# A linear-attention and feed-forward kernel: all chunks in pairs, decay folded into q and k, one written order for all work

## The chip, the cores and the metric

The kernel runs on one core of a Trainium2 chip. The core has five engines with an instruction queue each: PE (TensorE, matrix products into PSUM), DVE (VectorE), ACT (ScalarE), POOL (GpSimd) and SP (SyncE, which here only issues DMAs). Instructions of one engine run in the order of its queue; engines wait for each other through semaphores. The metric is the device time of one execution in microseconds (us). Before the change three runs took 216.35, 214.18 and 216.23 us, median 216.23.

## The reference

A causal attention without softmax, in which each head h forgets with a factor lam[h] per position, is followed by a two-layer network with ELU. The reference works in blocks of 64 positions; what it computes per head is

```python
intra = (qb @ kb.T) * Dmask          # Dmask[i, j] = lam ** (i - j) for i >= j, else 0
intra = intra @ vb
inter = (qb * lam_pow) @ kv_state    # lam_pow[i] = lam ** (i + 1)
out[block] = intra + inter
kv_state = lam ** block * kv_state + (kb * rev_pow).T @ vb   # rev_pow[j] = lam ** (block - 1 - j)
# then, with x = out as [3072, 512]:
h = x @ w_in                         # [3072, 2048]
g = where(h > 0, h, exp(min(h, 0)) - 1)
return g @ w_out                     # [3072, 512]
```

Batch 4, 8 heads, 768 positions, head size 64; inputs and output are float32, the kernel works in fp16 with float32 sums in PSUM.

## The kernel before, in words

The 3072 rows are 24 chunks of 128 positions: chunk g is position block g // 4 of batch g % 4. A chunk depends on the chunk four before it through the state of its batch.

For one chunk the program has these steps, each a small function. q, k and v are loaded by POOL's DMA queue with a cast to fp16 (`emit_load`, line 109), chunks 0 to 3 one by one, later ones two at a time; q of chunk 0 comes by SP's queue and is cast by DVE. T: q and k are transposed, for chunks 0 to 7 on PE (`att_T_pe`, 283), with q multiplied by the decay `qs` on its way out of PSUM (DVE, 290) and k copied by ACT (291); for later chunks by DMA transposes on SP's queue (`att_T_dma`, 268), straight from the loaded tiles. S: 16 matmuls give the scores (302). E: DVE multiplies them by `mask`, which holds the causal pattern and a decay per column (318). P: the values (338) and, from chunk 4 on, the state (344) are summed in PSUM, and ACT (359) or DVE (361) copies the result to `xt`. POOL makes the decayed k, `kd` (174), not for chunks 20 to 23. U: kd times v is the addition to the state (397 or 406); POOL has multiplied the old state by the block's decay into `stt` (378), and DVE adds the two (416, 418).

The network follows as units. mm1 of a group of chunks (`1:g:j`, line 478) puts 512 columns into one of two PSUM banks `psH`, then ACT writes exp into `e` (484) and relu in place (485); at the start of the next unit DVE makes g = min(e - 1, relu) (457). Chunks 0 to 3 are groups of one chunk: a unit has 16 matmuls of 128 columns and uses two of the eight pieces of w_in. From chunk 4 on a group has two chunks: 8 matmuls of 256 columns and one piece. mm2 (`2:g:j`, 499) sums four matmuls of 512 columns into the chunk's bank and uses two of the eight pieces of w_out; after four units ACT copies the chunk out and SP stores it. The last chunk keeps 128 columns for an extra step at the end (511).

The order around chunks 0 to 9 is written out by hand (`OPEN`), with 8 zero matmuls between (`w2`, `w6`); behind it a rule puts each pair's steps a fixed number of units ahead of its first use (`AT`), and up to two mm2 units behind each mm1 unit. POOL's own order up to chunk 10 is a list (`POOL_ORDER`): loads, weight pieces (i0 to i7 of w_in, o0 to o7 of w_out), kd (d) and state decay (m). PSUM banks are given to steps by name (`BANKS`).

Of the kernel before, what the change touches and what calls it, by code (L numbers as in the profile page):

```python
# [15 lines left out]
def kernel(  # L16
# [26 lines left out]
    GSIZE = {**{g: 1 for g in range(4)}, **{g: 2 for g in range(4, NG, 2)}}  # L43
# [3 lines left out]
    POOL_ORDER = (  # L47
        "k0 k1 iota q1 k2 v1 i0 v0 q2 i1 v2 i2 o0 i3 d0 q3 o1 i4 k3 i5 o2 o3 v3 d1 m4 d2 d3 i7 "
        "o4 o5 i6 o7 k4 o6 q4 m5 k6 v4 q6 k10 q10 d5 d4 d6 m6 v6 k8 q8 v8 d7 m7 v10"
    )  # L50
    RAW = "q0"
    FIRST = "q0:0 c0 c1 c2"
    OPEN = (
        "z1 z0 z3 Z1 Z2 Z0 z2 T0 w2 T1 S0 S1 w6 P0 P1 T2 1:0:0 S2 1:1:0 P2 U0 M 1:2:0 1:0:1 2:0:0 "
        "1:1:1 2:1:0 1:2:1 T3 2:2:0 1:0:2 S3 1:2:2 2:2:1 2:1:1 P3 1:1:2 1:3:0 2:0:1 2:0:2 "
        "2:1:2 1:1:3 U1 1:2:3 M Z3 2:2:2 1:3:2 U2 1:3:1 2:1:3 1:0:3 T5 T4 2:2:3 1:3:3 S4:5 "
        "2:0:3 2:3:2 2:3:0 M U3 M B:P4:P5:U4:U5 W8 2:3:3 1:4:1 T6 W9 1:4:0 T7 2:3:1 1:4:3 S6:7 "
        "1:4:2 2:4:0 2:5:0 1:4:5 1:4:4 2:4:1 B:P6:P7:U6:U7 1:4:7 1:6:1 2:5:2 2:5:1 1:6:0 1:4:6 "
        "2:4:2 S8:9 1:6:2 1:6:3 2:4:3 2:5:3 W11 W10 1:6:4 B:P8:P9:U8:U9 1:6:5 1:6:6 2:6:0 "
        "2:6:1 L12 1:6:7 2:6:2 1:8:0 S10:11 2:6:3 1:8:1 2:7:0 1:8:2 2:7:1"  # L60
    )
    LAGU = 7
    AT = {"L": -18, "W": -13, "T": -9, "S": -8, "B": -4}
    BANKS = (
        "S0=M0,M1 S1=C,D S2=D,M1 S3=D,B P0=M1 P1=B P2=B P3=D U0=M0 U1=D U2=A U3=M1 T0=M1,C "
        "T1=D,A T2=A,D T3=D T4=M0 T5=A T6=M1 T7=D M2=C M3=M0"
# [14 lines left out]
    def zero_matmuls(n):  # L81
# [4 lines left out]
    zero_matmuls(10)  # L86
# [4 lines left out]


# [3 lines left out]
    st = [  # L96
        [cpool.tile([128, NHP, 128], FP16, name=f"st{b}_{i}") for i in range(2)]
        for b in range(B)
    ]
    qg, kg, vg = {}, {}, {}  # L100

    def emit_load(w, g0):
        n = size_of[g0]
        c, b = divmod(g0, B)
        x = {"q": q, "k": k, "v": v}[w]
        src = x[b : b + n, :, c * L : (c + 1) * L].rearrange("b h p d -> p (b h) d")
        t = asb.tile([128, n, H, 64], FP16, tag=f"{w}n{n}", name=f"{w}n{g0}", bufs=4)
        {"q": qg, "k": kg, "v": vg}[w][g0] = t
        nc.gpsimd.dma_start(out=t[:].rearrange("p b h d -> p (b h) d"), in_=src)  # L109


    raw = {}
    for w in RAW.split():
        x = {"q": q, "k": k}[w[0]]
        g0 = int(w[1:])
        raw[w] = asb.tile([128, H, 64], FP32, name=f"raw_{w}", tag=f"raw_{w}")
        (nc.sync if w[0] == "q" else nc.scalar).dma_start(
            out=raw[w][:], in_=x[g0, :, 0:L].rearrange("h p d -> p h d")
        )
    nc.scalar.preload_act_table_set("natural_log_exp_and_others")  # L120

    def cast_raw(g, w, eng):
        n = f"{w}{g}"
        t = asb.tile([128, 1, H, 64], FP16, tag=f"{w}n1", name=f"{w}n{g}", bufs=4)
        (qg if w == "q" else kg)[g] = t
        if eng == 0:
            nc.vector.tensor_copy(t[:, 0], raw[n][:])
        else:
            nc.scalar.copy(t[:, 0], raw[n][:])

    def of(tiles, g):
        g0, i = group_of[g]
        return tiles[g0][:, i]
# [18 lines left out]

    def emit_wo(i):
        f0 = sum(WO[:i]) * 128
        nc.gpsimd.dma_start(  # L155
            out=wo16[i][:],
            in_=moe_w_out[f0 : f0 + WO[i] * 128, :].rearrange("(n p) f -> p n f", p=128),
        )

    iota_c = cpool.tile([128, 1], I32, name="iota_c")  # L160
    iota_r = cpool.tile([128, 128], I32, name="iota_r")

    def emit_iota():
        nc.gpsimd.iota(iota_c[:], pattern=[[0, 1]], base=0, channel_multiplier=1)
        nc.gpsimd.iota(iota_r[:], pattern=[[1, 128]], base=0, channel_multiplier=0)

    kds, qkT, Pt, psS, xg = {}, {}, {}, {}, {}

    def att_kd(g):
        if g // B == NCB - 1:  # L170
            return
        kd = asb.tile([128, H, 64], FP16, tag="kd", name=f"kd{g}", bufs=8)
        kds[g] = kd
        nc.gpsimd.tensor_tensor(  # L174
            out=kd[:], in0=of(kg, g),
            in1=ks[:].unsqueeze(2).broadcast_to([128, H, 64]), op=ALU.mult,
        )


    pool_list = POOL_ORDER.split()  # L180

    def emit_pool():
        w = pool_list.pop(0)
        if w == "iota":
            emit_iota()
        elif w[0] in "qkv":
            emit_load(w[0], int(w[1:]))
        else:
            {"i": emit_wi, "o": emit_wo, "d": att_kd, "m": lambda g: att_M(g)}[w[0]](int(w[1:]))

    def emit_pool_run():
        while pool_list and pool_list[0][0] != "m":
            emit_pool()

    assert "iota" in POOL_ORDER.split("d0")[0]
    while pool_list and pool_list[0][0] not in "dm":
        emit_pool()

    def zero_st1(b):
        nc.vector.memset(st[b][1][:], 0.0)  # L200


    loglam = cpool.tile([128, H], FP32, name="loglam")
    nc.scalar.activation(loglam[:], lam_b[:], AF.Ln)
    pos = cpool.tile([128, 3], FP32, name="pos")
# [4 lines left out]

    dn = cpool.tile([128, H], FP32, name="dn")
    mask = cpool.tile([128, H, 128], FP32, name="mask")
    qs = cpool.tile([128, NHP, 128], FP32, name="qs")
    ks = cpool.tile([128, H], FP32, name="ks")
    upp = cpool.tile([128, NHP], FP32, name="upp")
    nc.vector.tensor_copy(row[:], iota_r[:])
    nc.vector.tensor_copy(pos[:, 0:1], iota_c[:])
    nc.vector.tensor_scalar_mul(pos[:, 1:2], iota_c[:], -1.0)
    nc.scalar.activation(dn[:], loglam[:], AF.Exp, scale=pos[:, 1:2])
    nc.vector.tensor_scalar(  # L220
        out=ident16[:], in0=row[:], scalar1=pos[:, 0:1], scalar2=None, op0=ALU.is_equal
    )
    nc.vector.tensor_scalar(
        out=causT[:], in0=row[:], scalar1=pos[:, 0:1], scalar2=None, op0=ALU.is_ge
    )
    for hh in range(2):
        r = slice(hh * 64, (hh + 1) * 64)
        nc.vector.tensor_copy(loglam_p[r, :], loglam[r, hh::2])
    nc.vector.tensor_scalar_add(pos[:, 2:3], pos[:, 1:2], float(L))

    def emit_qs():
        for hp in range(NHP):
            nc.scalar.activation(
                qs[:, hp, :], row[:], AF.Exp, scale=loglam_p[:, hp : hp + 1]
            )

    def emit_mask():
        nc.vector.tensor_tensor(
            out=mask[:],
            in0=causT[:].unsqueeze(1).broadcast_to([128, H, 128]),  # L240
            in1=dn[:].unsqueeze(2).broadcast_to([128, H, 128]),
            op=ALU.mult,
        )

    def emit_ks():
        nc.scalar.activation(ks[:], loglam[:], AF.Exp, scale=pos[:, 2:3])
        nc.scalar.activation(upp[:], loglam_p[:], AF.Exp, scale=float(L))

# [13 lines left out]


    def att_T_dma(g):
        ts = []
        for w, tiles in (("q", qg), ("k", kg)):
            t = asb.tile([128, NHP, 128], FP16, tag=f"{w}T", name=f"{w}T{g}", bufs=6)
            nc.sync.dma_start_transpose(
                out=t[:], in_=of(tiles, g).rearrange("p h d -> p (h d)")
            )  # L270
            ts.append(t)
        qkT[g] = ts

    def att_T_pe(g):
        n = len(TAGS[f"T{g}"].split())
        pts = [
            bank(f"T{g}", i, [128, 2 // n, NHP, 128], FP16, f"psT{g}_{i}")
            for i in range(n)
        ]
        pts = [pts[0][:, 0], pts[n - 1][:, 2 // n - 1]]  # L280
        for src, pt in zip((of(qg, g), of(kg, g)), pts):
            for hp in range(NHP):
                nc.tensor.transpose(  # L283
                    pt[:, hp, :], in_=src[:, 2 * hp : 2 * hp + 2, :], identity=ident16[:]
                )
        qt, kt = [
            asb.tile([128, NHP, 128], FP16, tag=f"{w}T", name=f"{w}T{g}", bufs=6)
            for w in "qk"
        ]
        nc.vector.tensor_tensor(out=qt[:], in0=pts[0], in1=qs[:], op=ALU.mult)  # L290
        nc.scalar.copy(out=kt[:], in_=pts[1])  # L291
        qkT[g] = (qt, kt)

    def att_S(g):
        qt, kt = qkT[g]
# [11 lines left out]
    late, X_done, Y_done, E_done = [], set(), set(), set()  # L307

    def until(done, g):
        while g not in done:  # L310
            late.pop(0)()

    def att_E(g):
        pts = psS.pop(g)

        def half(hh):
# [5 lines left out]
            if hh == 1:  # L322
                E_done.add(g)
# [3 lines left out]
    def att_P(g):  # L327
        cb, b = divmod(g, B)
        until(E_done, g)
        if cb > 0:  # L330
            until(Y_done, g - B)
# [295 lines left out]
    for t in prog:  # L627
        run(t)
# [34 lines left out]
```

## Time and profile before

The profile is of one execution, whose span is 213.2 us between its first and last instruction; its own whole time is not listed. The median of the runs is 216.23, the fastest 214.18, so 1.0 to 3.0 us lie around the span.

| engine | busy us | share of the span | instructions |
|---|---|---|---|
| PE | 202.7 | 95% | 2066 |
| DVE | 130.1 | 61% | 224 |
| ACT | 129.0 | 61% | 245 |
| POOL | 96.2 | 45% | 115 |

| group (line) | count | busy us | mean ns |
|---|---|---|---|
| mm1, 256 columns (478) | 640 | 82.2 | 273 |
| mm1, 128 columns (478) | 256 | 17.1 | 220 |
| mm2, 512 columns (499) | 368 | 93.0 | 380 |
| g on DVE (457) | 96 | 65.8 | 686 |
| exp, relu on ACT (484, 485) | 192 | 114.3 | 595 |
| E on DVE (318) | 48 | 30.8 | 684 |
| kd on POOL (174) | 20 | 20.7 | 1040 |
| stt on POOL (378) | 32 | 19.5 | 608 |

A matmul's duration in the records includes its way through the array; matmuls in a row start closer together than they last, so the price of PE's work is read from the chain of waits, where each piece ends as the next begins. Load issues on POOL take its time as well: 1.1 us in the mean for q, k and v, 0.8 for w_in, 0.7 for w_out. A slice of the row view is 5.33 us; a digit is the busy share in tenths.

### The profile page before, as it was taken

How to read it: one execution, taken by the hardware profiler on the slowest of the kernel's cores; microseconds unless marked ns; L12 is line 12 of the kernel's file. 1: busy time of each engine (PE TensorE's matmuls, PEld its weight loads, DVE VectorE, ACT ScalarE, POOL GpSimd, SP SyncE). 2: the span in 40 equal slices, each digit the busy share in tenths (PEclk: the TensorE clock that was granted, in tenths of full speed). 3: DMA queues.
4: the chain of work that ended last, by engine and by line, in shares of the span. 5: the costliest groups of instructions: out<-in, count | busy, mean ns of one | idle time of the engine just before them, and what ended most of it. 6: DMA issues, size and time to landing. Idle time of an engine off the chain costs nothing.

```text
span 213.2 us, 5156 instructions
## 1 busy us (share of the span) xinstructions
PE 202.7 (95%) x2066; PEld 138.1 (65%) x2066; DVE 130.1 (61%) x224; ACT 129.0 (61%) x245; POOL 96.2 (45%) x115
## 2 busy tenths in 40 slices
PE   7667999999999999999999999999999999999994
PEld 2355676767686776766766766766766666666652
DVE  3936453777846888677667667667667547533321
ACT  4545654884867756676476476476476576477640
POOL 7996991999972908667166259300000000000000
PEclk9999999999999999999999999999999999999999
DMA  8999999999996999999939919999124110110112
GB/s 90 141 175 193 192 148 173 147 165 147 153 165 145 111 197 107 144 122 116 129 106 125 167 59 103 144 180 161 52 65 83 52 49 0 54 51 16 36 49 98
DMA packets 101976, 24.59 MB, mean 115 GB/s; under 512 B 92608, under 2 KB 99008, under 8 KB 101952
## 3 DMA queue, kind: packets, MB, share of 16 engines
q0 software_dynamic: 79760, 13.50, 83.1%
q1 hardware_dynamic: 22192, 10.76, 24.6%
q8 instruction: 16, 0.26, 0.5%
q14 instruction: 8, 0.07, 0.1%
HBM read 27.27 MB, written 6.29 MB: 157 GB/s over the span
## 4 chain that ended last, share of the span: by engine, by line
PE 82%; POOL 8%; DMA 7%; issue 1%; ACT 1%; DVE 0%; POOLq 0%; ACTq 0%
PE psM L499 36%; PE psH L478 35%; DMA wi<-in_moe_w_in_dram 4%; DMA wo<-in_moe_w_out_dram 3%; PE psO L338 3%; PE psS L302 3%; PE psO L344 2%; POOL kd L174 1%; POOL wi L148 1%; POOL kn L109 1%; POOL vn L109 1%; PE psU L406 1%; PE psT L283 1%; POOL qn L109 1%; POOL wo L155 1%
## 5 line engine op out<-in xcount | busy, mean ns | idle before, releaser
L478 PE MATMUL psH<-xt,wi 128*128 128x256 f16 (+1 forms) x896 | 99.3, 258 | 2.0 <-DMA wi<-in_moe_w_in_dram 1.1
L457 DVE SCALAR_TENSOR_TENSOR g<-e,psH 128x512 f16<-128x512 f32 x96 | 65.8, 686 | 56.7 <-ACT psH L485 56.0
L484 ACT ACTIVATE e<-psH 128x512 f32<-128x512 f32 x96 | 57.3, 597 | 65.0 <-PE psH L478 62.8
L499 PE MATMUL psM<-wo,g 128*128 128x512 f16 (+1 forms) x384 | 95.6, 377 | 0.7 <-DMA wo<-in_moe_w_out_dram 0.7
L478 PEld LDWEIGHTS <-wi 128*128 128x128 f16 x896 | 76.9, 98 | 27.4 <-DMA wi<-in_moe_w_in_dram 1.8
L485 ACT ACTIVATE psH<-psH 128x512 f32<-128x512 f32 x96 | 57.0, 593 | 0.0
L499 PEld LDWEIGHTS <-g 128*128 128x128 f16 x384 | 35.9, 98 | 29.3 <-issue 1.3
L318 DVE TENSOR_TENSOR pp<-psS,mask 128x512 f16<-128x512 f32 x48 | 30.8, 684 | 4.4 <-PE psS L302 4.4
L174 POOL TENSOR_TENSOR kd<-kn,ks 128x512 f16<-128x512 f16 x20 | 20.7, 1040 | 21.3 <-DMA kn<-in_k_dram 20.4
L378 POOL TENSOR_TENSOR stt<-st,upp 64x256 f32<-64x256 f16 x32 | 19.5, 608 | 14.7 <-DVE st L418 8.9
L109 POOL DMA_DIRECT2D vn<-in_v_dram x14 | 15.5, 1108 | 1.7 <-DMA wi<-in_moe_w_in_dram 1.7
L109 POOL DMA_DIRECT2D kn<-in_k_dram x14 | 15.5, 1105 | 0.8 <-POOLq L647 0.8
L525 ACT COPY osb<-psM 128x512 f32<-128x512 f32 x23 | 13.5, 590 | 3.2 <-PE psM L499 3.2
L109 POOL DMA_DIRECT2D qn<-in_q_dram x13 | 14.8, 1138 | 0.0
L418 DVE TENSOR_TENSOR st<-stt,psU 64x256 f16<-64x256 f32 x32 | 13.3, 416 | 1.2 <-PE psU L406 0.5
L361 DVE TENSOR_TENSOR xt<-psO,qs 128x512 f16<-128x512 f32 x16 | 11.0, 688 | 3.5 <-PE psO L344 3.5
L338 PE MATMUL psO<-pp,vn 128*64 128x128 f16 x192 | 12.0, 222 | 1.2 <-DMA vn<-in_v_dram 1.0
L338 PEld LDWEIGHTS <-vn 128*64 128x64 f16 x192 | 9.7, 110 | 4.6 <-issue 2.9
L344 PE MATMUL psO<-qT,st 128*64 128x128 f16 x160 | 10.0, 219 | 0.0
L344 PEld LDWEIGHTS <-st 128*64 128x64 f16 x160 | 8.9, 110 | 0.0
L302 PE MATMUL psS<-qT,kT 64*128 64x128 f16 x192 | 7.9, 218 | 0.3 <-ACT kT L291 0.3
L359 ACT CAST xt<-psO 128x512 f16<-128x512 f32 x8 | 4.4, 588 | 6.4 <-PE psO L338 4.3
(44 smaller groups left out, 72.3 us busy)
## 6 DMA issues: line engine op xcount, KB each, us to landing
out_dram<-osb SPq DMA_DIRECT2D x23, 256.0 KB, 2.2
kn<-in_k_dram POOLq DMA_DIRECT2D x10, 256.0 KB, 7.8
qn<-in_q_dram POOLq DMA_DIRECT2D x10, 256.0 KB, 6.8
vn<-in_v_dram POOLq DMA_DIRECT2D x10, 256.0 KB, 7.6
wi<-in_moe_w_in_dram POOLq DMA_DIRECT2D x8, 256.0 KB, 6.9
wo<-in_moe_w_out_dram POOLq DMA_DIRECT2D x8, 256.0 KB, 7.7
kn<-in_k_dram POOLq DMA_DIRECT2D x4, 128.0 KB, 4.2
vn<-in_v_dram POOLq DMA_DIRECT2D x4, 128.0 KB, 5.5
```

Source lines behind the costliest of these rows:

```text
L109: nc.gpsimd.dma_start(out=t[:].rearrange("p b h d -> p (b h) d"), in_=src)
L174: nc.gpsimd.tensor_tensor(out=kd[:], in0=of(kg, g), in1=ks[:].unsqueeze(2).broadcast_to([128, H, 64]), op=ALU.mult,)
L302: nc.tensor.matmul(psS[g][hh][:, hp, :], lhsT=kt[r, hp, :], rhs=qt[r, hp, :], start=True, stop=True,)
L318: nc.vector.tensor_tensor(out=P[:], in0=pts[hh][:], in1=mask[:, hh::2, :], op=ALU.mult)
L338: nc.tensor.matmul(po[r, hp, :], lhsT=vt[:, 2 * hp + hh, :], rhs=Pt[(g, hh)][:, hp, :], start=True, stop=(cb == 0), skip_group_check=True,)
L344: nc.tensor.matmul(po[r, hp, :], lhsT=st[b][cb % 2][:, hp, r], rhs=qt[:, hp, :], start=False, stop=True, skip_group_check=True,)
L378: nc.gpsimd.tensor_tensor(out=tmp[r], in0=old[r, :, r], in1=upp[r].unsqueeze(2).broadcast_to([64, NHP, 64]), op=ALU.mult,)
L457: nc.vector.scalar_tensor_tensor(out=g[:].rearrange("p f c t -> p (f c t)"), in0=e[:], scalar=-1.0, in1=r[:], op0=ALU.add, op1=ALU.min,)
L478: nc.tensor.matmul(pH[:, f * n * 128 : (f + 1) * n * 128], lhsT=wi16[i][:, kk, w * 128 : (w + 1) * 128], rhs=xg[g0][:, kk, :], start=(kk = ...
L484: nc.scalar.activation(e[:], pH[:], AF.Exp)
L485: nc.scalar.activation(pH[:], pH[:], AF.Relu)
L499: nc.tensor.matmul(psM[g][:, cols], lhsT=gts[(g, j * FB + f)], rhs=wo16[i][:, w, cols], start=first and f == 0, stop=end and f == FB - 1, ...
```

## The change

Chunks 0 to 3 become groups of two as well, so every mm1 unit has 8 matmuls of 256 columns and needs one piece of w_in. POOL's load order is now k0 k1 i1 q1 k3 v0 q3 k2 v1 q2 i0 v3 v2 i3 o0 o1 q4 i2 k4 i4 o2 o3 i5 i7 q6 v4 i6 k6 o5 o4 o7 o6 and then pairs. The decayed k (`kd`) is transposed and used for the scores too, k carries lam^(128 - j) and q, or from chunk 8 on the result, lam^(i - 128); so E multiplies by a causal pattern alone, and chunks 20 to 23 have a kd as well. kd of chunks 0 to 3, 17 and 23 is made on DVE. The state is kept with its decay: DVE adds (y), then POOL multiplies (m). U of chunks 0 to 3 takes the 64-column form. The zero matmuls in the middle are gone. exp and relu are steps of their own (h), as g is, and the planner is replaced by one list for all engines.

```diff
-    GSIZE = {**{g: 1 for g in range(4)}, **{g: 2 for g in range(4, NG, 2)}}
+    GSIZE = {g: 2 for g in range(0, NG, 2)}
-    RAW = "q0"
-    FIRST = "q0:0 c0 c1 c2"
+    RAW = "q0S"
+    ORDER = (
+        "L:k0 L:k1 i:1 log logp iota col L:q1 row ks qn ident qs:1 qs:3 a:q0:v z:1:0:a L:k3 z:3:0:a d:0:v "
+        "t:q0 qs:2 e:q0:a L:v0 d:1:v t:k0 e:k0:a z:0:1:v t:k1 caus L:q3 qs:0 s:0 e:k1:a E:0:1 L:k2 E:0:0 t:q1 "
...
+        "E:2:1 L:q4 E:2:0 u:3 h:0:0 p:3 g:0:1 p:2 i:2 u:2 y:0 L:k4 x:2:v 1:0:3 g:0:0 x:3:a i:4 1:2:1 h:0:3 "
+        "o:2 h:2:1 o:3 g:0:3 2:0:0 i:5 z:2:1:a 1:2:0 g:2:1 i:7 y:2 t:q4 h:2:0 t:q5 L:q6 1:2:3 z:1:1:v 2:1:0 "
...
+        "o:7 E:5:1 2:2:1 h:2:5 E:5:0 o:6 1:2:7 g:2:5 s:4 h:2:7 2:0:1 L:q8 E:4:1 1:0:7 g:2:7 E:4:0 t:q7 L:k8 "
...
+        "s:6 d:9:p D:k8 E:7:1 1:4:0 E:6:0 L:k18 1:4:3 D:k9 h:4:0 E:7:0 E:6:1 u:4 L:q14 u:6 p:7 h:4:3 y:4 p:6 "
+        "g:4:0 u:7 d:12:p u:5 2:2:3 y:5 m:5 D:k12 1:4:2 g:4:3 x:6:a 1:4:6 h:4:2 d:11:p x:7:v 2:3:3 d:10:p "
+        "D:k11 g:4:2 s:9 s:8 y:6 1:6:6 L:v10 h:4:6 D:k10 E:8:0 2:4:1 E:9:1 h:6:6 m:4 D:q10 g:4:6 2:4:0 g:6:6 "
+        "L:q12 1:6:0 D:q11 E:9:0 1:4:4 d:13:p y:7 h:6:0 E:8:1 u:8 p:9 m:7 D:k13 h:4:4 g:6:0 u:9 p:8 1:6:5 x:8 "
+        "L:k16 g:4:4 2:4:3 h:6:5 x:9 s:11 s:10 z:2:0:a E:11:1 1:8:5 m:6 E:10:1 2:5:2 h:8:5 g:6:5 L:q16 E:10:0 "
...
+        "2:22:1 h:20:5 g:22:6 2:21:1 g:20:5 2:23:3 2:22:3 2:21:2 2:20:2 R"
     )
...
+    def att_kd(g, eng="p"):
+        kd = asb.tile([128, H, 64], FP16, tag="kd", name=f"kd{g}", bufs=8)
+        kds[g] = kd
+        {"v": nc.vector, "p": nc.gpsimd}[eng].tensor_tensor(
+            out=kd[:], in0=of("k", g),
+            in1=ks[:].unsqueeze(2).broadcast_to([128, H, 64]), op=ALU.mult,
+        )
+    def att_T_dma(w, g):
+        t = asb.tile([128, NHP, 128], FP16, tag=f"{w}T", name=f"{w}T{g}", bufs=6)
+        src = of("q", g) if w == "q" else kds[g][:]
+        nc.sync.dma_start_transpose(out=t[:], in_=src.rearrange("p h d -> p (h d)"))
+    def att_E(g, hh):
+        P = asb.tile([128, NHP, 128], FP16, tag="pp", name=f"pp{g}_{hh}", bufs=6)
+        nc.vector.tensor_tensor(
+            out=P[:], in0=psS[g][hh][:],
+            in1=causT[:].unsqueeze(1).broadcast_to([128, NHP, 128]), op=ALU.mult,
+        )
+    def att_M(g):
+        new = stp[b][(cb + 1) % 2]
+        for hh in range(2):
+            nc.gpsimd.tensor_tensor(out=new[r, :, r], in0=stt.pop((g, hh))[r], in1=upp[r]..., op=ALU.mult)
+    def att_Y(g, hh):
+        if cb == 0:
+            nc.vector.tensor_tensor(out=stp[b][1][r, :, r], in0=src, in1=upp[r]..., op=ALU.mult)
+        else:
+            nc.vector.tensor_tensor(out=tmp[r], in0=stp[b][cb % 2][r, :, r], in1=src, op=ALU.add)
```

The letters of the list: L load, i and o weight pieces, a and d decayed q0 and k, t and e transposes on PE and their copies, D transposes by DMA, s scores, E mask, p and x values and their copy, u, y, m state, `1:g:j` mm1, h exp and relu, g the ELU's last step, `2:g:j` mm2, z zeroing, R the last columns; a trailing a, v or p names ACT, DVE or POOL. Every engine gets its own steps in this order.

## The prediction

> **What bounds the kernel now.** I read the 40 slices first, then the chain of waits in order of time, then the timeline of the first 45 us, and last the landings of single transfers.
>
> ```profile
> span 213.2 us, 5156 instructions
> PE   7667999999999999999999999999999999999994
> DVE  3936453777846888677667667667667547533321
> POOL 7996991999972908667166259300000000000000
> ```
>
> PE (TensorE) is full from the fifth slice on; only the first four (21 us) and the last are not. So the change can gain in the head, or lose by opening gaps behind it. The chain prices PE's work (columns: start, length, line, matmuls):
>
> ```profile
> 36.89 0.89 PE psH L478 x16
> ...
> 52.52 0.87 PE psH L478 x8
> 53.40 0.45 PE psT L283 x8
> 53.84 0.86 PE psM L499 x4
> ...
> 55.58 0.55 PE psS L302 x16
> ```
>
> An mm1 unit costs 0.89 us with 16 matmuls of 128 columns and 0.87 with 8 of 256; an mm2 unit 0.86 (0.65 for the last chunk's 384 columns); the transposes of one chunk's q and k 0.45; scores of two chunks 0.55. A later part of the same chain has P of a chunk in 0.45 (eight pairs of matmuls with the values and eight with the state at 0.056 a pair; 0.22 where there is no state yet) and U of two chunks in 0.25; the first four U, of 128 columns, take 0.22 each. Before: 16 x 0.89 + 80 x 0.87 + 92 x 0.863 + 4 x 0.65 + 8 x 0.45 + 12 x 0.55 + 9.9 (P) + 2.9 (U) + 0.9 (last columns) = 189.7 us. PE ends at 210.1, so 20.4 us are not work. At 45.3, where the scores of chunks 4 and 5 start, 29.0 us of work are done: 16.3 us of the 20.4 lie ahead of that point. The other 4.1 are about 0.32 per pair of chunks (a first mm2 unit behind scores takes 0.97 instead of 0.86, a burst of P opens 0.12 late) and one stall of 0.5 us near 87.
>
> What ends the gaps in the head are transfers:
>
> ```profile
> 20.46 0.62 PE L478 MATMUL psH<-xt,wi 128*128 128x128 f16 x8 [0.66 <-DMA wi<-in_moe_w_in_dram]
> 20.70 0.89 POOL L109 DMA_DIRECT2D vn<-in_v_dram  x1 [1.66 <-DMA wi<-in_moe_w_in_dram]
> ...
> 21.88 0.59 PE L499 MATMUL psM<-wo,g 128*128 128x512 f16 x2 [0.36 <-DMA wo<-in_moe_w_out_dram]
> ...
> 34.26 1.46 PE L499 MATMUL psM<-wo,g 128*128 128x512 f16 x6 [0.35 <-DMA wo<-in_moe_w_out_dram]
> ```
>
> The second line is POOL itself: its ninth load back has to land before it issues the next, eight are in flight. Issue plus time to landing, load by load, gives one line of landings almost without gaps from 5.3 to 41.8 us: a q, k or v of one chunk every 0.85 (v2 at 15.2, behind a weight at 14.35), a w_in piece 1.35 to 1.45, a w_out piece 1.2, a pair's q or k 1.75. In the head the load queue is the bound.
>
> **The change, part by part.**
>
> *Shapes.* The 256 narrow mm1 matmuls become 128 wide ones: 16 x 0.02 = 0.3 us. U of chunks 0 to 3 in the 64-column form: 4 x (0.22 - 0.125) = 0.4. Work after: 189.0. The 8 zero matmuls that go lay in waits: nothing.
>
> *Loads, the head.* POOL issues the same 11 chunk loads, seven w_in and four w_out pieces, with q and k of pair 4 among them. Before had landed these 22 at 30.4, so the 24 land by 30.4 + 2 x 1.75 = 33.9; POOL's stall of 1.66 and its five kd and stt operations between loads go, but the queue was full beside them, so I credit nothing. Backwards from 33.9: w_in 7 at 33.9, w_in 5 at 32.5, w_out 3 at 31.1, w_in 4 at 28.7; forwards from 5.3: v1 13.4, q2 14.3, w_in 0 15.7, v2 17.4, w_in 3 between 18.8 and 20, w_out 1 at 21.2. Now PE's order is walked along these. q2 is transposed at 14.4; unit 1:0:1 starts at 14.6, 1:0:0 at 16.2; DVE needs 0.6 us an operation (the spacing of neighbours in its timeline), and has E of chunk 2, the first g, y0 and x2 in a row until 19.9; 1:0:3 and 1:2:1 fit there, and 2:0:0 starts at 21.4 with 7.8 us of work done. From there DVE and PE run side by side: ten g, six y halves and three copies out of PSUM for nine units, 0.1 to 0.3 us late at some of them. 1:2:5 waits for w_in 5 at 32.5 (19.0 done: 13.5 idle), then for g and E until 1:0:6 starts at 39.5 with 25.1 done. That is 14.4 idle, and 14.6 at 29 us of work, against 16.3: **1.7 us gained**. Bounds: 2.9 if the two hitches of 1.2 us in before's landings (17.9 to 20.4, 30.4 to 33.0) stay away; 0 if DVE, which has some 14 us to do from 14.6 to 32, is 0.2 later than walked at each of nine units. Iota now stands behind w_in 1 on POOL, 0.75 later: q0 is transposed at 5.9 instead of 5.6, hidden by k1 and q1, which land at 6.3 and 8.8.
>
> *kd once.* q and k now carry the decay, so the mask is only causal; E keeps its form and its 0.68 us. Chunks 20 to 23 need kd as well, and six kd go to DVE: 24 - 6 = 18 x 1.04 on POOL instead of 20. On DVE a kd is not seen before; nearest are 0.67 (cast of q0) and 0.69 (state add is 0.42 for half): 0.65, six times, four of them in the head's walk above. But the transposes of k by DMA now wait for POOL's kd, where they waited for the load: on SP's queue the transposes of q and the stores stand behind them.
>
> *State.* y (DVE) and then m (POOL, 2 x 0.61) instead of stt and then add: the same operations, with POOL now last before P. Nearest is the old stt, which waited up to 4.9 us for DVE and delayed nobody on PE; the order leaves 2.8 us of PE's work or more between m and P: nothing, at most 0.5.
>
> *Order behind the head.* Transitions between forms stay about 10 for scores and 10 for P and U: 3.5 us as before, without the 0.5 at 87. But scores of chunks 6 to 13 now fall between 36 and 61 us of work (before 39 to 78). From 36 to 66 I count 14 g, 16 E, 6 x (0.6 to 0.67 each) and 6 y of two halves (0.85): 27.4 to 28.7 us of DVE in 30; on POOL nine loads of 1.17, nine kd of 1.03 and six m of 1.28: 27.5. Walking 17 us of it, 2:5:2 starts 0.9 late, 0.4 of it transitions: 0.5, for the stage **0.8 us**. Then the transposes for chunks 10 and 11: m5 waits for y5 (56.7 us), behind it on POOL stand kd11 and kd10, then SP issues k11, k10, q10, q11 at 1.22 to 1.3 each; q11 leaves at 63 to 64 and the scores are due at 66.5. One lands 2.4 us after issue alone and 7.4 beside three loads (the answers for the transposes at 94.6 and 76.8): a stall of 0 to 3.5. I take 4.4, the value at 97.2 beside one or two loads: **0.8**. The same queue for chunk 12, and v14, whose load is issued 8 us ahead: 0 to 1 each, taken as 0.
>
> *exp apart from mm1.* With two psH buffers a unit can start 3.0 us after the one two ahead of it (0.87, 0.26 to ACT, 1.1 for exp and relu, 0.7 for g). In the new order eight of 94 stand closer in PE's work: three in the head, which the walk has, five by 0.1: nothing more, 0.5 if ACT is behind its copies.
>
> *End.* Chunks 20 to 23 now finish within 3 us, four stores together where the last ones stood 2 us apart: 0 to 1, taken as **0.4**.
>
> Sum: 189.0 + 14.6 + 3.5 + 0.8 + 0.8 = 208.7 for PE's end, 1.4 ahead of 210.1; less 0.4: span 212.2. The three runs of before have 214.18 to 216.35, the profiled execution 213.2 with 1.0 to 3.1 around it; against the median the forecast is 216.2 - 1.0 = **215.2 us**.
>
> **A rule that speaks against it.** The first ten zero matmuls start 0.43 us apart, the six at 9.57 0.22, with the granted clock shown at 1.00 throughout; those six and two more kept PE busy in the head's waits and go. The Trainium skill, TensorE: Matmul & The Clock Gate, Part 1, says that PE runs at half its clock until a window of about 3.4 us was busy, and falls back after an idle one; the first ten agree with it, a fall back is not in this trace.
>
> **The rivals.**
> 1. *Late transposes and kd (slower).* Place: SP's and POOL's queues from 48 to 80 us. It decides once q11 lands more than 2.5 us after its issue. At 7.4 the stall is 3.5 instead of 0.8 (+2.7), the same queue costs 1 at chunk 12, DVE waits 1.5 instead of 0.8 (+0.7) behind scores that come in a heap, and the last stores 1 instead of 0.4: 5.0 above the forecast, 220.2; half of it gives 217.7. For it: three of the twenty transposes that I read took 5.4 to 7.4 beside loads; against: eight took under 2.8.
> 2. *The loads come as their queue alone would bring them.* Head 2.9 gained, no stall at the scores, 0.3 on DVE, no store late: 215.2 - 1.2 - 0.8 - 0.5 - 0.4 = 212.3. For it: from 21 to 29 us landings had no hitch; against: POOL and DVE are fuller than before.
> 3. *Half speed in the head.* PE has some 3.2 us of matmuls between 5.9 and 14.6 us. If that lets the pace of the first ten return, the 3.2 us of work from 14.6 to 18.1 take 6.4; 0.7 to 1.9 of that are hidden, as w_in 3 lands at 18.8 to 20, and E, y and x on DVE hide more: 0.5 to 2.5 on top, 215.7 to 217.7.
> 4. *Nothing.* The pairing itself removes 0.3 us, and the bound is PE: head and later stalls cancel, 216.2.
>
> **How the numbers follow.** A measurement of this kernel tells about 1% (2.2 us) from no change. Forecast with case 4: 0.40, own range 213.5 to 217.5. Case 2: 0.33, between 210.5 and 214. Case 1: 0.20. Case 3: 0.07. Faster by over 1% (under 214.0) is case 2 and a little of the forecast's lower edge: 0.37. Slower by over 1% (above 218.4) is most of case 1 and a bit of 3: 0.22. Between: 0.41. The range for 8 in 10 goes from case 2's lower end to short of case 1's full price: 210.5 to 219.5.
>
> **What would show it.** PE's share in the first four slices up, and 1:0:6 at 39 to 40 us; w_in 7 landing near 34; a gap on PE ahead of the scores of chunks 10 and 11 at 66 to 70, released by the transposes or by their copies; E, g and x back to back on DVE from 48 to 80; the last stores 2 us or more apart from PE's end. It is wrong if the landings between 14 and 34 us move by over 1 us, or if PE waits for POOL's m.

## The result and the profile after

The changed kernel takes 222.61 us in the median of four runs, the kernel before 215.65 beside it: a ratio of 1.034, 95% interval 1.028 to 1.040. The forecast was 215.2, in a range of 210.5 to 219.5. It is slower, and outside the range. The profiled execution is one of 222.63 us with a span of 220.9. Medians below are of executions in the faster of two states; one in the slower state, 225.39 us of the run with far loads later and kd first, is left out.

The row view of the page after the change, 40 slices of 5.52 us, with the clock row added (the TensorE clock that was granted, in tenths of full speed):

```profile
span 220.9 us, 4883 instructions
PE   7489899999995599999999999999999999999994
DVE  3787687764895457859377835487785544433230
POOL 7998786968397366285942402002060000000000
PEclk9758999999999679999999999999999999999999
```

The clock row of the kernel before:

```profile
PEclk9999999999999999999999999999999999999999
```

Two things are new: a hole in PE at slices 13 and 14, and a clock that is not full in slices 2 to 4 and again in 14 and 15. The table of windows gives the clock its times (columns: stretch, its length, busy us of PE, weight loads, DVE, ACT and POOL with counts, granted clock, DMA share, GB/s):

```profile
5.00:10.00 5.00, 2.63 (x26) 1.47 (x25) 3.63 (x8) 3.48 (x10) 5.00 (x7) 0.82 1.91 149
10.00:15.00 5.00, 3.39 (x48) 2.67 (x47) 4.36 (x8) 1.28 (x3) 5.00 (x7) 0.50 2.19 165
15.00:20.00 5.00, 5.00 (x60) 3.50 (x57) 3.08 (x7) 2.48 (x5) 5.00 (x7) 0.65 1.65 189
60.00:70.00 10.00, 9.17 (x114) 6.08 (x112) 8.52 (x15) 6.47 (x13) 8.80 (x11) 1.00 1.77 174
70.00:75.00 5.00, 0.98 (x17) 0.81 (x17) 0.33 (x1) 0.00 (x0) 3.40 (x4) 0.81 1.78 125
75.00:80.00 5.00, 5.00 (x18) 2.40 (x17) 4.18 (x8) 1.09 (x2) 0.74 (x2) 0.51 2.45 156
80.00:100.00 20.00, 20.00 (x234) 14.31 (x233) 13.34 (x24) 12.32 (x24) 12.52 (x14) 1.00 1.44 147
```

PE's timeline shows both prices in single instructions (start, length, line, matmuls, idle before and what ended it):

```profile
16.37 1.91 PE L451 MATMUL psH<-xt,wi 128*128 128x256 f16 x8
...
68.14 1.03 PE L475 MATMUL psM<-wo,g 128*128 128x512 f16 x4
74.02 1.03 PE L328 MATMUL psS<-qT,kT 64*128 64x128 f16 x16 [4.86 <-DMA qT<-qn]
74.99 1.89 PE L451 MATMUL psH<-xt,wi 128*128 128x256 f16 x8
76.67 3.49 PE L475 MATMUL psM<-wo,g 128*128 128x512 f16 x8
```

An mm1 unit that lasts 1.04 us elsewhere lasts 1.91 at 16.37 and 1.89 at 74.99; two mm2 units take 3.49. In between PE stands still for 4.86 us before the scores of chunk 11 (the list has 11 ahead of 10), until the DMA transpose of q11 has landed. The chain of waits tells what made it late (start, length, what):

```profile
53.63 2.48 DVE pp L335 x4
56.11 0.32 DVE stt L402
...
57.94 0.43 DVE stt L402
...
58.38 0.61 POOL stp L386
...
59.75 2.04 POOL kd L275 x2
61.80 1.16 POOL vn L159
...
62.97 0.64 POOL stp L386
63.61 0.44 SPq L297
...
64.14 1.32 SPq L297
...
65.51 8.37 DMA qT<-qn
...
74.02 1.03 PE psS L328 x16
```

DVE has four masks (E of chunks 7 and 6, line 335) ahead of y5 (402); POOL's m5 (386) waits for y5, the decayed k of chunks 11 and 10 (275) stand behind m5, and SP issues k11, k10, q10, q11 in order; q11's transpose then needs 8.4 us. (The load of v10 and the state's step for chunk 4, 61.80 to 63.61 in the chain, run beside this: by SP's timeline k11 leaves at 60.82, k10 at 62.75 and q10 right behind it at 64.14.) Another condition is hidden here: the load of q10, issued at 44.8, takes 18.5 us and lands at 63.3, 0.8 us before its transpose leaves.

For the account I take, at scores of a chunk, the start on PE less the PE work counted ahead of it: the idle or slow time so far. At chunk 7 it is 17.0 (the kernel before has 16.6 at as much work), at 11 it is 22.8, at 12 26.0, at 23 27.6, and 28.5 at PE's end, where the kernel before had 20.4.

### The profile page after: what moved, and what is told of

The parts are those of the page before. It is cut to its first block, busy times and chain, and to the rows that moved or that the text cites. A ratio compares the mean times of both kernels' runs of the same rounds, so it can differ in the third digit from the quotient of the medians.

```text
span 220.9 us, 4883 instructions
## 1 busy us (share of the span) xinstructions
PE 206.0 (93%) x1946; PEld 138.8 (63%) x1946; DVE 133.6 (60%) x232; ACT 126.6 (57%) x241; POOL 94.4 (43%) x113
## 4 chain that ended last, share of the span: by engine, by line
PE 77%; DVE 8%; DMA 5%; ACT 3%; POOL 2%; issue 1%; SPq 1%; ACTq 0%; POOLq 0%
PE psM L475 34%; PE psH L451 33%; DMA qT<-qn 4%; PE psS L328 3%; DVE pp L335 3%; PE psO L349 2%; DVE g L436 2%; PE psO L355 1%; DMA lam_b<-in_lam_dram 1%; DVE stt L402 1%; DVE stp L396 1%; PE psTk L304 1%; PE psU L419 1%; DVE qT L313 1%; POOL kd L275 1%
## 5 line engine op out<-in xcount | busy, mean ns | idle before, releaser
L451 PE MATMUL psH<-xt,wi 128*128 128x256 f16 x768 | 98.0, 276 | 1.4 <-ACT psH L462 1.2
L475 PE MATMUL psM<-wo,g 128*128 128x512 f16 (+1 forms) x384 | 93.1, 382 | 0.1
L451 PEld LDWEIGHTS <-wi 128*128 128x128 f16 x768 | 74.1, 99 | 23.1 <-DVE g L436 2.0
L386 POOL TENSOR_TENSOR stp<-stt,upp 64x256 f16<-64x256 f32 x32 | 19.5, 609 | 59.1 <-DVE stt L402 49.5
L335 DVE TENSOR_TENSOR pp<-psS,causT 128x512 f16<-128x512 f32 x48 | 31.4, 684 | 10.9 <-PE psS L328 10.6
L275 POOL TENSOR_TENSOR kd<-kn,ks 128x512 f16<-128x512 f16 x18 | 18.5, 1043 | 4.1 <-issue 2.9
L159 POOL DMA_DIRECT2D qn<-in_q_dram x13 | 14.6, 1122 | 1.9 <-DMA qn<-in_q_dram 1.9
L402 DVE TENSOR_TENSOR stt<-stp,psU 64x256 f32<-64x256 f16 x32 | 13.3, 414 | 0.5
L328 PEld LDWEIGHTS <-kT 64*128 64x128 f16 x192 | 6.5, 103 | 10.9 <-issue 10.2
L355 PE MATMUL psO<-qT,stp 128*64 128x128 f16 x160 | 10.6, 219 | 0.0
L355 PEld LDWEIGHTS <-stp 128*64 128x64 f16 x160 | 9.0, 110 | 0.0
```

The lines of the kernel that those rows point to most:

```text
L275: {"v": nc.vector, "p": nc.gpsimd}[eng].tensor_tensor(out=kd[:], in0=of("k", g), in1=ks[:].unsqueeze(2).broadcast_to([128, H, 64]), op=ALU ...
L328: nc.tensor.matmul(psS[g][hh][:, hp, :], lhsT=kt[r, hp, :], rhs=qt[r, hp, :], start=True, stop=True,)
L335: nc.vector.tensor_tensor(out=P[:], in0=psS[g][hh][:], in1=causT[:].unsqueeze(1).broadcast_to([128, NHP, 128]), op=ALU.mult,)
L355: nc.tensor.matmul(po[r, hp, :], lhsT=stp[b][cb % 2][:, hp, r], rhs=qt[:, hp, :], start=False, stop=True, skip_group_check=True,)
L386: nc.gpsimd.tensor_tensor(out=new[r, :, r], in0=stt.pop((g, hh))[r], in1=upp[r].unsqueeze(2).broadcast_to([64, NHP, 64]), op=ALU.mult,)
L451: nc.tensor.matmul(pH[:, f * n * 128 : (f + 1) * n * 128], lhsT=wi16[i][:, kk, w * 128 : (w + 1) * 128], rhs=xg[g0][:, kk, :], start=(kk = ...
```

## The experiments

The theories: (1) loads needed only much later (k18, q14, v12), the far loads, fill the transfers' queue and hold the transposes up; rivals: POOL's wait for y5, the transfers as a whole, or DVE's order; (2) the sparse matmuls in the head let the clock fall, at 2.4 us; rival: loads and DVE set the head's end anyway. All runs beside each other; ratios are to runs of the kernel before on the same chip, which had medians of 214.57 to 215.65:

| run | us | ratio, 95% interval | at chunk 7 | 11 | 12 | 23 |
|---|---|---|---|---|---|---|
| changed kernel | 222.61 | 1.034 (1.028 to 1.040) | 17.0 | 22.8 | 26.0 | 27.6 |
| warm head | 221.02 | 1.026 (1.022 to 1.030) | 14.6 | 21.1 | 24.3 | 26.0 |
| far loads later | 221.75 | 1.026 (1.018 to 1.034) | 16.9 | 21.9 | 23.9 | 26.7 |
| both | 219.83 | 1.020 (1.015 to 1.024) | 14.8 | 20.3 | 22.3 | 25.1 |
| filled stall | 220.39 | 1.023 (1.019 to 1.027) | 16.4 | 21.8 | 22.8 | 24.8 |
| kd first | 221.23 | 1.030 (1.027 to 1.033) | 16.9 | 22.4 | 24.4 | 26.2 |
| far loads later and kd first | 218.43 | 1.016 (1.012 to 1.020) | 17.0 | 19.6 | 19.9 | 23.4 |
| near things first | 219.77 | 1.026 (1.020 to 1.032) | 16.0 | 18.8 | 19.6 | 24.5 |
| chunks 8, 9 transposed on PE | 219.76 | 1.024 (1.016 to 1.031) | 17.5 | 22.0 | 24.0 | 25.7 |
| scores later | 218.88 | 1.019 (1.017 to 1.022) | 17.0 | 19.5 | 20.2 | 23.8 |
| scores later, g ahead | 218.65 | 1.020 (1.015 to 1.024) | 16.9 | 18.6 | 19.7 | 23.1 |
| that, warm head | 218.47 | 1.016 (1.011 to 1.020) | 15.5 | 20.8 | 21.9 | 24.5 |
| that, v14 and scores 8, 9 moved | 216.53 | 1.008 (1.005 to 1.011) | 14.9 | 17.5 | 18.6 | 21.1 |

The last four columns are of the profiled execution of each. The edits are in the written list; besides it, only names of banks, a parameter that lets the zero matmuls use another bank, and a condition for transposing chunks 8 and 9 on PE were changed.

### The head's clock

```diff
-t:k0 e:k0:a ... s:0 ... t:q1 ... t:q3
+t:k0 w:3 e:k0:a ... s:0 w:4 ... t:q1 w:4 ... t:q3 w:4
```

> The changed kernel with 15 zero matmuls put back into the waits of its head (3 behind k0's transposes, 4 each behind the scores of chunk 0, the transposes of q1 and those of q3). If the sparse matmuls of the head let the clock fall: granted clock 1.00 through the head, unit 1:0:1 in 1.04 us instead of 1.91, PE 2 to 2.5 us earlier at the scores of chunk 7 (51.0 instead of 53.2). What is left of it at the end depends on the stall before the scores of chunks 10 and 11: if the transfers set its end (73.9), the stall grows to some 7 and the time stays at 222 (221.5 to 222.7); if it hangs on PE's own earlier work by way of the state, all moves forward: 220.2. Rival, no effect of the clock on the end of the head because loads and DVE set it: scores of chunk 7 at 53 as now, time 222.6.

221.02. The windows of this run have the clock at 1.00 (columns as above), and what ends PE's wait in the head is a load again:

```profile
5.00:10.00 5.00, 4.55 (x35) 2.13 (x34) 3.93 (x9) 3.53 (x10) 5.00 (x7) 1.00 2.03 157
10.00:15.00 5.00, 4.90 (x74) 3.01 (x73) 5.00 (x10) 2.19 (x5) 5.00 (x8) 1.00 2.09 160
```
```profile
15.98 1.05 PE L451 MATMUL psH<-xt,wi 128*128 128x256 f16 x8
...
19.28 2.01 PE L451 MATMUL psH<-xt,wi 128*128 128x256 f16 x16 [1.31 <-DMA wi<-in_moe_w_in_dram]
```

The scores of chunk 7 come at 50.8 instead of 53.2: 2.4 us, as expected. One execution of the same head can differ from another: nine traces without these zero matmuls have 16.0 to 17.5 us at chunk 7, seven with them 14.6 to 15.5, so the two groups do not meet. Behind the scores of chunk 7, 1.2 go in a wait for k9's transpose, and the stall is still 4.2. So theory (2) holds for the head; of the 2.4 us 1.6 are left at the end, between the two cases that were named.

The same was asked of the kernel before, in which `w2` and `w6` were taken out of `OPEN`:

> The kernel before without its eight zero matmuls behind the first ten (two after the transposes of chunk 0, six after the scores of chunk 1). If sparse matmuls in the head let the clock fall in any order of the work: granted clock near 0.5 from about 9 to 17 us, 0.5 to 2 us slower, 216 to 217.5. If the head of that kernel waits for transfers anyway, the clock falls and the time stays: 215.4. If the clock does not fall, the zero matmuls are not what kept it up.

214.58 against 215.05, ratio 0.998 (0.997 to 1.000): not slower. The clock falls here as well:

```profile
10.00:15.00 5.00, 2.39 (x30) 2.23 (x31) 1.97 (x4) 1.40 (x3) 4.93 (x7) 0.50 1.91 171
```

Its P of chunk 0 waits 3.1 us for v0 and starts at 12.6, and the scores of chunks 4 and 5 come at 44.8 as against 45.3. In these two heads half speed costs where PE is the last to be ready, and nothing where a load is.

### The stall: far loads

```diff
-L:q10 L:v12 ... L:k18 ... L:q14 ... L:v10 ... L:q12 ... L:k16 ... L:q16 ... L:k22 ... L:k14 ... L:q18
+L:q10 ... L:v10 ... L:q12 ... L:v12 ... L:q14 ... L:k16 ... L:k14 ... L:q16 ... L:q18 ... L:k18 L:v20 L:k22
```

with the decayed k and the transposes of chunks 14 to 19 and 22 moved back likewise.

> The changed kernel with the loads of work that lies far ahead moved back in the list (k18, q14, v12, k16, q16, k22, and with them the decayed k and the transposes of chunks 14 to 19 and 22). If these loads are what keeps the transposes of chunks 10 and 11 waiting: q10 lands before 60 instead of at 63.3, the transposes of q11 some 3 to 5 us after their issue, no stall before the scores, no half clock behind it: 4.9 + 2.9 off, 214.8 (214 to 217). If POOL's own queue was the cause (the state's last step for chunk 5 waits 4.15 us there, two kd behind it), only the two loads that no longer stand ahead of it count: 2 us off at most, 220.5. If DVE is behind by itself, the gap comes back as waits for E and g: 217 to 219.

221.75, a gain that is not clear of the noise (the intervals 1.018 to 1.034 and 1.028 to 1.040 overlap). The stall is 4.0. The load queue runs empty at 62 to 64 us, so the far loads are gone; but q10 still lands only at 62.7 instead of 63.3, m5 starts at 58.0, and q11's transpose is issued at 65.3, nearly as in the changed kernel, and takes 7.7. Theory (1) as I had it falls. With the warm head:

> Both edits, the zero matmuls in the head and the far loads later. If both causes are real and the transfers no longer set the pace: 222.6 - 7.8 - 2.4 = 212.4, below the kernel before. If the head's gain is lost again where DVE or a load comes late: as with the later loads alone, about 215.

219.83, well above both cases: by the ratios 1.4% for both edits, 0.8% for each alone, and together they leave a stall of 3.3.

### The stall: half clock behind it

```diff
-x:9 s:11
+x:9 w:18:M0 s:11
```

> The changed kernel with 18 zero matmuls (18 x 0.22 = 4.0 us) in the stall before the scores of chunk 11, in a bank that is free there. If the half speed between 74 and 79 us comes from PE standing still: the stall's end stays at 73.9, the clock is 1.00 behind it, 2.9 us off: 219.7. If the clock falls there for another reason: 222.6, or up to 1 more where the zero matmuls run over.

220.39, 1.0% less. PE's timeline:

```profile
68.40 4.05 PE L121 MATMUL psZ<-zero 128*128 128x512 f16 x18
73.04 0.62 PE L328 MATMUL psS<-qT,kT 64*128 64x128 f16 x16 [0.59 <-DMA qT<-qn]
73.60 1.05 PE L451 MATMUL psH<-xt,wi 128*128 128x256 f16 x8
74.48 1.89 PE L475 MATMUL psM<-wo,g 128*128 128x512 f16 x8
```

The scores come no earlier than the transposes let them, but the two mm2 units behind take 1.89 instead of 3.49. From the scores of chunk 11 to those of chunk 12 it loses 1.0 instead of 3.2, so 2.2 are gained, where I had expected 2.9. Of the 1.0, 0.6 is a new wait for a g at 83.6: the half clock itself had taken 2.8. That the standstill brings it is shown.

### The stall: two limits at the same time

```diff
-y:5 m:5 D:k12 ... d:11:p ... d:10:p D:k11
+y:5 D:k12 ... d:11:p ... d:10:p m:5 D:k11
```

> The changed kernel with POOL's decayed k of chunks 11 and 10 ahead of the state's step for chunk 5, which waits 4.15 us for DVE; nothing else moves. If that wait on POOL is what sends the transposes of chunks 10 and 11 late: k11 and k10 leave at 56 to 58 instead of 60.8 and 62.8, q10 and q11 as soon as q10 has landed (63.3), alone with the loads: q11 lands at 69 to 71 instead of 73.9, 3 to 5 us off the stall and up to 2.9 off the half clock: 215 to 219. If the transfers as a whole are what is full (nine transposes and seven loads in 24 us): q11 still lands at 73 or later, 222.

221.23. k11 and k10 now leave at 56.1 and 59.2, but the chain goes through the load of q10:

```profile
45.15 19.31 DMA qn<-in_q_dram
...
64.47 1.19 SPq L297
...
65.72 7.78 DMA qT<-qn
...
73.63 0.86 PE psS L328 x16
```

q11 lands at 73.5, as the rival had it. In the changed kernel two limits on the time at which q10's transpose can leave ended within a microsecond of each other: the chain behind POOL's wait at 64.1 and q10's load at 63.3. With the first one gone, the second sets the same time. Both edits, this one and the far loads later:

> The changed kernel with the far loads later and the decayed k of 11 and 10 ahead of the state's step, the two edits that gave 0.9 and 1.4 us alone. If POOL's wait and the full transfers are two limits that end at about the same time, so that removing one shows the other: more than the sum, q11 lands at 68 to 71, the stall at 0 to 2 and little half clock: 216.5 to 218.5. If they are small causes beside a third: the sum, 220.3, and a stall of 3 or more.

218.43. The stall is 1.6 and there is no slow stretch behind it. At chunk 12 it has lost 19.9, 6.1 less than the changed kernel, where the two alone had saved 2.1 and 1.6. (1.8 us come back at 113 us, where U of chunks 14 and 15 waits; the trace names a kd there, in the run with the far loads later alone it was the load of v14, 1.0.) What is left of the stall is again the load and the transposes beside it:

```profile
45.27 18.25 DMA qn<-in_q_dram
...
63.54 1.19 SPq L297
...
64.78 5.87 DMA qT<-qn
...
```

q10 still lands at 63.5, and q11's transpose leaves only 0.7 us earlier than in the changed kernel. So it is not a limit on leaving that has gone: 2.5 of the 3.3 us are q11's time to land, 5.9 instead of 8.4, where one edit alone had left 7.8 or 7.7. k11 and k10 have gone ahead and the far loads are not beside it; why it takes both edits is not shown further.

With q10 ahead in the queue as well (`L:k10 L:q10 L:v8 L:k12` for `L:k12 L:k10 L:v8 L:q10`, and chunks 11 and 10 ahead of 12 among the kd and the transposes):

> The changed kernel with the far loads later, as in the earlier run, and what chunks 10 and 11 need ahead of what chunks 12 and 13 need: loads k10 and q10 before k12, the decayed k of 11 and 10 before the state's step and before that of 12, the transposes k11, k10, q10, q11 before k12. If the transfers are full until the stall (loads and transposes together) and only their order is wrong: q10 lands 5 us or more earlier, q11's transpose at 66 to 69, the stall under 1 and no half clock behind it, 222.6 - 7 = 215.5; some of it may come back at chunks 12 and 13 (up to 4: then 218 to 219). If the transfers of chunks 8 to 11 alone are already too many for the time, the stall stays at 3 or more: 221.

219.77. Here both limits on leaving are gone: q10 lands at 54.6, q11's transpose at 65.0, and there is no stall. In its place PE waits elsewhere:

```profile
PE psU L419 <- DMA vn<-in_v_dram: 2.2, 1, 2.2
PE psO L355 <- POOL stp L386: 1.7, 3, 1.0
...
PE psS L328 <- DMA qT<-qn: 0.9, 1, 0.9
```

(columns: who waited for what, total us, times, longest). POOL now meets k12's load, which lands at 63.9, and the state's steps stand behind that kd. Last, are the transposes themselves a load on the transfers? q and k of chunks 8 and 9 on PE:

```diff
-D:q8 D:q9 D:k8 D:k9
+t:k8 e:k8:a ... t:q8 e:q8:v ... t:k9 e:k9:a ... t:q9 e:q9:v    (scores of 8, 9 two units later)
```

> The changed kernel with q and k of chunks 8 and 9 transposed on PE (4 x 0.225 us of PE's work, four copies on ACT and DVE) instead of by DMA; the scores of 8 and 9 stand two units later. If DMA transposes take the transfers' time like loads do (2 to 2.8 us each), four of them away bring q11 8 to 11 us earlier: no stall, no half clock, 222.6 - 7.8 + 0.9 = 215.7. If only the loads fill the queue, q11 moves by less than 2 us and the time stays at 221 to 222.

219.76, with two runs at 218.2 and 218.6 and two at 221.0 and 221.3, of which the last was profiled; so the size of the gain is unclear. Its trace answers the question: q10's load takes 11.3 us instead of 18.5 and lands at 56.5, 6.8 us earlier. That is 1.7 us for each of the four transposes, an estimate from this one pair of traces, and as much as a pair's load. But m5 still starts at 58.9 and q11 leaves at 66.0: POOL's limit, seen alone.

### The due time

```diff
-x:9 s:11 s:10 ... p:10 ... p:11 ... 1:8:7 ... 1:6:4 ... 1:6:1 ... s:12 ... s:13 ... 1:6:7 ... p:13 ... p:12
+x:9 ... 1:8:7 ... 1:6:4 ... s:11 s:10 ... 1:6:1 ... p:10 ... p:11 ... 1:6:7 ... s:12 s:13 ... 2:7:0 ... p:13 ... p:12
```

(bank B instead of A for one half of the scores of chunk 11; y9 ahead.)

> The changed kernel with the scores of chunks 10 and 11 6.4 us of PE's work later in the list and those of 12 and 13 some 5 later, with their mask, values and state additions; loads, decayed k and transposes stay where they are. If nothing but the due time of these scores is wrong (the transposes come as early as the queues can bring them): no stall, no half clock behind it, 4.9 + 2.9 off: 214.8, up to 1 more if q13 lands after 84. If the late scores only push the wait on to the P of these chunks or to DVE: 217 to 219.

218.88: no stall and no slow clock behind it, without a transfer moved. It is 4 us more than expected and in the range of the rival: PE waits three times for g, 3.5 us in all, and two of these waits, 1.1 at 75 and 1.7 at 89 us, stand in the stage that was moved, where g stood behind masks and state additions on DVE. With g ahead of them and mm2 units between:

> As the run with later scores, but with g ahead of the mask and an mm2 unit between the mm1 units where PE waited 3.5 us for g. If those waits came only from where the steps stood in DVE's order: 218.9 - 3 = 216 (215.5 to 217). If DVE or the transfers are full there anyway: 218 to 219.

218.65: the waits for g fall to 1.8, of which 0.9 stand in the head, and 0.7 us of idle are gained in its profiled execution; by the medians it is about the same, and the expected 216 did not come. The order of DVE's steps did cause these waits; in their place PE waits 0.8 for the load of v14. DVE was busy for 31 of the 40 us from 60 to 100, so it is not full there.

### Together

> Four edits on the changed kernel: zero matmuls in the head, the far loads later, the decayed k of 11 and 10 ahead of the state's step, and the scores of chunks 10 to 13 later. If the head's clock (2.4 us) and the stall with its half clock (7.8) are all that separates forecast and result: 212.4, below the kernel before. If the transfers of the whole first half set the pace, the gap only moves: 215 to 218.

219.41, ratio 1.021 (1.018 to 1.024), above both cases. With the clock at 1.00 throughout, PE waited 2.8 for g, 1.7 for w_in (in the head) and 1.6 for a v at 114 us. Then with near things first and all scores moved:

> Zero matmuls in the head, far loads later, near ones first, v14 earlier, the scores of chunks 8 to 13 one to six units later, and g, mask and mm2 rearranged around them so that no unit has to wait for the g of the unit two before it. If head clock, transfers and the DVE waits of the earlier run with later scores (3.5 us) are all that is lost: idle of PE some 15 at the scores of chunk 7 and 18 to 19 at the end instead of 27.6: 212 to 214, at or below the kernel before. If each stage gives back what the one before has gained: 217.

219.77, ratio 1.023 (1.019 to 1.027), above both cases. P waited 1.9 for POOL at 66 to 68 us, where m5 was now behind two kd; the clock was 0.50 behind these waits, from 68 to 71; and mm1 waited 1.5 for x at 19.7, in the head. So with fewer edits:

> The run with later scores and g ahead of the mask, with the 15 zero matmuls in the head: nothing else. If the head's clock and the due time of the scores are two separate losses: 218.65 less the 1.6 to 2.4 that the zero matmuls gave alone: 216.3 to 217.1. If the earlier PE only meets the transfers of chunks 8 and 9 or 10 and 11 earlier: 218 to 218.7.

218.47: as the second case had it. In the profiled execution (219.47, the slowest of four) PE waited 2.0 for k9's transpose, and the clock fell behind this wait too:

```profile
61.62 0.85 PE L328 MATMUL psS<-qT,kT 64*128 64x128 f16 x16 [2.00 <-DMA kT<-kd]
62.40 1.89 PE L451 MATMUL psH<-xt,wi 128*128 128x256 f16 x8
```

It was 0.50 from 62 to 65 us, and what the head had won was gone.

> The same, and two small edits: the scores of chunks 8 and 9 two units later (PE waited 1.2 us for k9's transpose there in the run with zero matmuls alone), and v14 and v20 exchanged among the loads (0.8 us of waiting for v14). If these waits are lost time of their own: 2 us below the run without them, 214.5 to 215.5, level with the kernel before. If the time only moves to the next wait: no change against it.

216.53, ratio 1.008 (1.005 to 1.011): 1.9 us below the run without the two edits, as expected, though that run itself had come out higher than its forecast, and 6.1 below the changed kernel. The clock is 1.00 throughout. The last version takes y10, y12 and a mask out of the way of three g by putting them behind, and y8 by putting it one unit earlier:

> The last run (zero matmuls, later scores, v14 earlier) with the three g for which PE still waited 0.2 to 0.5 us moved ahead of the state additions y8, y10, y12 and of one mask on DVE. If these waits, some 0.9 us with the restart of PE, are time of their own: 216.5 - 0.9 = 215.6, within 1% of the kernel before. If DVE only passes them on: 216.5.

217.28, ratio 1.012 (1.007 to 1.017): not the 215.6 that was hoped for, and not clearly different from the version before it. The waits were 1.5 instead of 0.9, of which 1.3 now stand at 93 to 100 us, behind the moved additions. No version beat the kernel before.

## Why the prediction was wrong

PE's end was forecast at 208.7 and came at 217.5, in the terms: head +2.4, stall +4.1, half clock behind it +2.2, the rest +0.1.

*The head.* The step was right except for the clock. With full clock PE had lost 14.3 at the scores of chunk 4 (21 us of work) and 14.6 at those of chunk 7 (36 us), and the forecast has 14.6 at 29; w_in 5 and 7 landed at 31.5 and 32.9, a microsecond ahead of the forecast. The zero matmuls "lay in waits: nothing" was the error: they cost nothing and kept the clock. This was rival 3, priced at 0.5 to 2.5 and given 0.07, although the forecast had itself counted 3.2 us of work in the 8.7 us from 5.9 to 14.6. That the kernel before runs as fast without them shows that the time is not in the zero matmuls as such but in who is last: the new order made PE last.

*The transposes for chunks 10 and 11.* This is the term that was mis-sized: 0.8 forecast, 4.9 measured, and this was rival 1, given 0.20, beyond its own price of 3.5. The chain was seen (m5 behind y5, kd11 and kd10 behind it, four issues on SP) and its times were nearly right (q11 away at 63 to 64, measured 65.5). What failed is the time to land: 4.4 was taken from before's lightly loaded 97 us, while in this stage it was 8.4. The two rows of before, at 76.8 and at 97.2 us:

```profile
qT<-qn SPq DMA_TRANSPOSE x1, 7.4
...
qT<-qn SPq DMA_TRANSPOSE x1, 4.4
```

q11's departure and PE's arrival at the scores (69.2 for 66.5) both came some 2 us late, so the 4.0 us of landing are nearly all of the 4.1. The landing had to be read where loads and transposes compete; before's 7.4 was the nearer row. Nor was the load of q10 priced at all: it was the second limit, and removing POOL's wait alone brought q11 only 0.4 us forward.

*What a stall does to the clock.* No term stood for it: 2.2 us net, shown by the filled stall. Rival 1 and rival 3 were two cases in the forecast, but the same gate joins them.

*Right.* The work (189.0); kd on DVE at 0.65 (0.68); that DVE costs little between chunks 7 and 9 (0.6 of 0.8); the end (0.3 more tail for 0.4); the later stage, which lost 2.5 from chunk 12 on. PE never waited directly for POOL's m in the changed kernel: m's harm was to what stood behind it. What is not settled is the last 1.3 us between the best version and the kernel before; PE's 0.9 us of waits for g are part of it, and the one attempt to remove them only moved them.

## What to carry to other kernels

Take a transfer's time to land from the stage whose queues are as full as where it will go, and price a stall with the slow clock that follows it. When the removal of one cause yields a fraction of the stall, look for a second limit that ends at the same time, and try edits together before a theory is dropped. If something arrives late and its use can wait, moving the use in the order is the cheaper edit; but count what the engine that serves it already has there.

## What the runs showed of the hardware

Half clock needs no long wait. In the head of the changed kernel the clock fell between 8.0 and 8.5 us and stood at 0.50 until 18.5. Since the first ten zero matmuls no wait of PE had been longer than 1.0, but PE had been busy only 1.2 of the 3 us from 5 to 8; from 10 to 15 it was busy 3.39 of 5 us by its own (slowed) records, and the clock stayed low. Later, a wait of 2.00 us (the run with later scores, g ahead and warm head) and one of 2.19 (chunks 8 and 9 transposed on PE) were followed by half clock, while one of 2.16 at 114 us (near things first) and one of 1.75 at 113 us (far loads later and kd first) were not: the length of the wait alone does not decide it in these runs. The Trainium skill, TensorE: Matmul & The Clock Gate, Part 1, names an idle window of about 3.4 us for the fall; the stall of 4.9 us agrees, the head and the waits of 2.00 and 2.19 us do not. Part 4 says that transposes on PE don't count as busy in the same way; that fits the head, where many matmuls are transposes, but no run separates them.

In one pair of traces a DMA transpose took the transfers' time like a load of twice its size: four of 128 KB removed brought q10's load 6.8 us forward, 1.7 each, and a pair's load that writes 256 KB takes 1.75. The Trainium skill, Advanced Engine Details and Errata, section X-Bar Transpose, calls such transposes as fast as regular DMAs; by this estimate they were half as fast per byte written, and beside loads the transpose of q11 took 5.9 to 8.4 us from issue to landing, where one alone took 2.4 in the kernel before.
